# A linear-attention and MLP kernel: batch loads issued after the rest transposes, k loaded ahead of q at the start, group 0's output tiles copied by ScalarE

## The chip, the cores and the metric

The kernel runs on one core of one Trainium2 chip. The metric is the device time of one execution in microseconds; of several runs the median counts. A profiled execution gives the trace from which all durations below are read. Line numbers (L349) are those of the kernel's source. PE is TensorE, DVE is VectorE, ACT is ScalarE, POOL is GpSimd, SP is SyncE; SPq and ACTq are the queues on which SP and ScalarE issue DMAs.

## The reference

Linear attention over 8 batches, 8 heads, 576 positions and a head size of 64, followed by a two-layer MLP over the 4608 tokens (model size 512, inner size 2048):

```python
def phi(x):
    return np.where(x > 0, x, np.exp(x) - 1.0) + 1.0
q_p, k_p = phi(q), phi(k)
kv  = einsum('bhsd,bhse->bhde', k_p, v)
z   = sum(k_p, axis=2)
num = einsum('bhsd,bhde->bhse', q_p, kv)
den = einsum('bhsd,bhd->bhs', q_p, z)[..., None] + 1e-06
x   = (num / den) -> [B * S, H * D]
h   = x @ w_in
out = gelu_tanh(h) @ w_out
```

Inputs and output are float32 in HBM.

## The kernel before

**Tiling.** Each batch of 576 positions is split into a main part of 512 (`MAIN`, four chunks of 128, `C = 4`) and a rest of 64. The main parts of the 8 batches are 8 groups of the MLP (`iteration(j)`, j = 0 to 7). The rests of two batches 2m and 2m + 1 share a tile of 128 (m = 0 to 3), and the four of them make a ninth group (j = 8, `xt_rest`). Batches 0 and 1 (`PAIRED`) take all 576 positions of k and v in one layout; from batch 2 on, the rest keys and values are tiles of their own (`kr`, `vr`), and the rest queries are `qr` for all m.

**What a batch needs before its group.** `exp_of` (ScalarE), `linear_of` and `least_of` (DVE) make phi of q and k; v is cast to bfloat16. `kv_main` or `kv_paired` multiplies k and v on TensorE into `kv_ps`, which `kv_evac` copies to `kvbd`. q is transposed into `qt`. `nab` then multiplies `qt` and `kvbd` into `n_ps` and divides (reciprocal L307, product L309, both on DVE) into x; the tile `n_ps` has one buffer, so one n waits until DVE has read the one before. x is transposed into `xt`. From batch 2 on the transposes of q and x are DMAs on SP's queue (L543, L576), as are those of the rests (`qtr` L589, `xt_rest` L603); for batches 0 and 1 TensorE transposes and ScalarE copies.

**Order.** It is written by hand. A group has 32 slots: 16 h steps (`h_mm`, 4 matmuls, then gelu on ScalarE), then 16 o steps (4 matmuls each into `o_ps`). `at(j, slot, fn)` files work of other batches behind a slot of group j, and `run` emits it there, in the order of filing within a slot. Each engine, and each DMA queue, executes in the order emitted. For a batch b of 4 or more: loads at (b - 3, 18) (for b = 4 at (1, 29)), linear at (b - 2, 13) and after, exp at (b - 2, 15), `least_q` with its four transposes at (b - 2, 17), kv at (b - 1, 2), n at (b - 1, 4), 6, 8 and 10. For the rests m = 1 to 3: load at (2m - 1, 18), exp at (2m, 15), `least` with the transpose `qtr` at (2m, 22), and n at slot 2 of group 4, 5 or 7. So in group 4 the queue of SP gets, in this order, the q transposes of batch 6, the loads of batch 7 (q, k, v, 1 MB each) and the transpose of the rest queries m = 2, whose n stands at (5, 2). The loads of an even batch have four more DMAs, for `kr` and `vr`.

**The start.** SP issues halves of q, k, q, k and then v of batch 0, and behind them the weights. `first_batch` makes phi half by half in the same order, keeps TensorE's clock up with matmuls on a zero tile (`keep_warm`), transposes q on TensorE in two pieces that ScalarE copies to `qt`, and goes on through kv, n, x and the first quarters of h.

**The output.** `finish` copies a tile of 128 x 512 from `o_ps` into half of `o_sb` (`evac`: by DVE for even t, by ScalarE for odd t, in group 0 t = 3 by DVE); a store of 512 KB goes out on ScalarE's queue for each two tiles. In group 0 the o steps run u by u, so the four tiles finish in slots 28 to 31, among the n, the x transposes and the first h quarters of batch 1; its second store is filed at (1, 2).

Of the kernel before, what the change touches and what calls it, by code (L numbers as in the profile page):

```python
# [15 lines left out]
def kernel(  # L16
# [15 lines left out]
    nc = tc.nc  # L32
# [5 lines left out]
    C = 4  # L38
# [35 lines left out]
    def bank(name, shape, dt=FP32):  # L74
        return ps_b.tile(shape, dt, name=name, tag="b")
# [9 lines left out]
    def ld_tile(name, b):  # L85
        shape = [P, NP, J * D] if b in PAIRED and name != "q" else [P, H, C * D]
        ld[name, b] = pld.tile(shape, FP32, name=name + "_x", tag="ld")

    def load_pairs(name, src, b, us=slice(0, NP)):
        s = src[b].rearrange("h s d -> (h s d)").rearrange("(u n f) -> n u f", n=P, f=J * D)  # L90
        nc.sync.dma_start(out=ld[name, b][:, us, :], in_=s[:, us, :])  # L91

    def load_q_paired(b, parities=(0, 1)):
        src = q[b, :, 0:MAIN, :].rearrange("(u a) (p c) d -> p a u (c d)", a=2, c=C)
        for a in parities:
            nc.sync.dma_start(out=ld["q", b][:, NP * a : NP * (a + 1), :], in_=src[:, a])
# [39 lines left out]
    def cast_w_in(i, fn, fs=slice(0, 512)):  # L136
        fn(
            out=w_in_sb[:, :, 512 * i + fs.start : 512 * i + fs.stop],
            in_=w_st[True, i][:, :, fs],
        )  # L140
# [8 lines left out]
    halves = (slice(0, 2), slice(2, 4))  # L149
    for n in "qkv":  # L150
        ld_tile(n, 0)
    for s in range(2):
        load_q_paired(0, (s,))
        load_pairs("k", k, 0, halves[s])
    for s in range(2):
        load_pairs("v", v, 0, halves[s])
    for i in range(4):
# [42 lines left out]
    def by_chunk(t, hs):  # L200
        return t[:, :, hs, :].rearrange("p c h d -> p h c d")

    def phi_tiles(name, b):
        n, hn = ld[name, b].shape[2] // D, ld[name, b].shape[1]
        phi[name, b] = pphi.tile([P, n, hn, D], BF16, name=name + "_p")

    def exp_of(name, b, hs=None):
        x = ld[name, b]
        hs = hs or slice(0, x.shape[1])
        if (name, b) not in exps:  # L210
            exps[name, b] = pe.tile([P, x.shape[2] // D, x.shape[1], D], BF16, name=name + "_e")
        nc.scalar.activation(  # L212
            by_chunk(exps[name, b], hs),
            x[:, hs].rearrange("p h (c d) -> p h c d", d=D),
            AF.Exp,
        )

    def linear_of(name, b, hs=None):
        x = ld[name, b]
        hs = hs or slice(0, x.shape[1])  # L220
        if (name, b) not in phi:
            phi_tiles(name, b)
        nc.vector.tensor_scalar(  # L223
            by_chunk(phi[name, b], hs),
            x[:, hs].rearrange("p h (c d) -> p h c d", d=D),
            1.0,
            1.0,
            op0=ALU.add,
            op1=ALU.max,
        )  # L230

    def least_of(name, b, hs=None):
        p, e = phi[name, b], exps[name, b]
        if hs:
            p, e = p[:, :, hs, :], e[:, :, hs, :]
        nc.vector.tensor_tensor(p, p, e, op=ALU.min)  # L236
# [3 lines left out]
    def cast_v_paired(b, us, fn):  # L240
        fn(
            out=vp_paired(b)[:, :, us, 0:D].rearrange("p j u d -> p u j d"),
            in_=ld["v", b][:, us].rearrange("p u (j d) -> p u j d", d=D),
        )
# [12 lines left out]
    def kv_paired(b, ii, kv_of):  # L257
        kp, vp = phi["k", b], vp_paired(b)
        for j in range(J):
            for s in range(2):  # L260
                for a in range(2):
                    r, u = slice(HP * a, HP * (a + 1)), 2 * ii + s
                    nc.tensor.matmul(  # L263
                        kv_of(a, ii)[HP * s : HP * (s + 1)],
                        lhsT=kp[r, j, u, :],
                        rhs=vp[r, j, u, :],
                        start=(j == 0),
                        stop=(j == J - 1),
                        skip_group_check=True,
                    )  # L270
# [16 lines left out]
    def kv_evac(b, blocks, src, fn):  # L287
        for s in range(2):
            r = slice(HP * s, HP * (s + 1))
            fn(out=kvbds[b % 4][r, blocks, E * s : E * (s + 1)], in_=src[r])  # L290
# [78 lines left out]
    def xt_chunk(j, c):  # L369
        return xts[j][:, :, P * c : P * (c + 1)]  # L370

    def gelu_table():
        nc.scalar.preload_act_table_set("gelu_apprx_tanh_and_others")  # L373
# [3 lines left out]
    def first_batch():  # L377
        w_ps = bank("w_ps", [P, 512])

        def keep_warm(n):  # L380
            for _ in range(n):
                nc.tensor.matmul(w_ps, lhsT=warm[:, 0:P], rhs=warm)  # L382

        qt = pt.tile([P, C, NP, P], BF16, name="qt")
        qs = (slice(0, 4), slice(4, 8))

        def transpose_q(s, fn):
            t_ps = bank("t_ps", [P, C, 2, P], BF16)
            for i in range(2):
                for c in range(C):  # L390
                    h = 4 * s + 2 * i
                    nc.tensor.transpose(
                        t_ps[:, c, i, :], phi["q", 0][:, c, h : h + 2, :], ident
                    )
            fn(out=qt[:, :, 2 * s : 2 * s + 2, :], in_=t_ps)

        keep_warm(18)
        for s in range(2):
            exp_of("q", 0, qs[s])
            exp_of("k", 0, halves[s])  # L400
            linear_of("q", 0, qs[s])
            least_of("q", 0, qs[s])
            linear_of("k", 0, halves[s])
            least_of("k", 0, halves[s])
        transpose_q(0, nc.scalar.copy)
        keep_warm(10)
        transpose_q(1, nc.scalar.copy)
        keep_warm(2)
        for ii in range(2):
            cast_v_paired(0, halves[ii], nc.vector.tensor_copy)  # L410
        for ii in range(2):
            kv_ps = [bank("kv_ps", [P, E]) for _ in range(2)]
            kv_paired(0, ii, lambda a, ii: kv_ps[a])
            for a, fn in enumerate((nc.vector.tensor_copy, nc.scalar.copy)):
                block = slice(2 * a + ii, 2 * a + ii + 1)
                kv_evac(0, block, kv_ps[a].rearrange("p (i e) -> p i e", i=1), fn)
        gelu_table()
        for s in range(2):
            cast_w_in(0, nc.gpsimd.tensor_copy, slice(256 * s, 256 * s + 256))
        for i in range(1, 4):  # L420
            cast_w_in(i, nc.gpsimd.tensor_copy)
        for i in range(2):
            cast_w_out(i, nc.gpsimd.tensor_copy)
        cast_w_out(2, nc.gpsimd.tensor_copy, slice(0, 2))
        keep_warm(2)

        xts[0] = pt.tile([P, NP, MAIN], BF16, name="xt")
        x = {0: nab(qt[:, 0], 0), 1: nab_in_banks(qt[:, 1], 0)}
        for c in range(C):
            transpose_x(x[c], xt_chunk(0, c), nc.scalar.copy)  # L430
            if c + 2 < C:
                x[c + 2] = (nab, nab_in_banks)[c % 2](qt[:, c + 2], 0)
            if c > 0:
                h_quarter(0, c - 1, 3)
        h_quarter(0, C - 1, 3)

    first_batch()


# [3 lines left out]
    def at(j, slot, fn, *args):  # L443
        j, slot = j + slot // 32, slot % 32
        fill.setdefault((j, slot), []).append((fn, args))
# [160 lines left out]
        at(j, s_least, least)  # L606
        at(j_n, 2, n)

    def evac(dst, src, t):
        if t % 2 == 0:  # L610
            nc.vector.tensor_copy(dst, src)  # L611
        else:
            nc.scalar.copy(dst, src)  # L613

    def store_rest(t, o_sb, fs, engs):
        for s in range(2):
# [7 lines left out]
    def finish(j, t, o_ps):  # L624
        if j == B:
            o_sb = pout.tile([P, 2, d_model], FP32, name="o_sb")
            evac(o_sb[:, 0, :], o_ps, t)
            store_rest(t, o_sb, slice(0, d_model), (nc.scalar, nc.sync))
            return
        if t % 2 == 0:  # L630
            o_sbs[j, t // 2] = pout.tile([P, 2, d_model], FP32, name="o_sb")
        o_sb = o_sbs[j, t // 2]
        evac(o_sb[:, t % 2, :], o_ps, 0 if j == 0 and t == C - 1 else t)
        if t % 2 == 1:
            ov = out[j * S : j * S + MAIN, :].rearrange("(p c) f -> p c f", c=C)[:, t - 1 : t + 1]

            def store():
                nc.scalar.dma_start(out=ov, in_=o_sb)

            if j == 0 and t == C - 1:  # L640
                at(1, 2, store)
            else:
                store()
# [65 lines left out]
    for b in range(4, B):  # L709
        plan_prepare(b, (b - 2, 13), (b - 2, 15))  # L710
        if b > 4:
            at(b - 3, 18, load_batch, b)
    for m in range(1, 4):
        at(2 * m - 1, 18, load_rest, "qr", q, m)
        plan_rest(m, 2 * m, 15, 22, (4, 5, 7)[m - 1])
# [37 lines left out]
```

## Time and profile before

| | us |
|---|---|
| median of 3 runs | 298.3 |
| lowest, highest | 298.05, 299.46 |
| the profiled execution | 299.1 |
| its span, first to last instruction | 297.3 |
| TensorE busy (matmul) | 279.2 |
| ScalarE busy | 163.8 |
| DVE busy | 109.2 |
| mean granted clock of TensorE | 0.981 |

The span stands for what the instructions take; 1.8 us of the execution lie outside it. "Busy" is the time in which an engine has an instruction in work. The waits name who waited for whom, with the total, the number and the longest. The chain of work is followed back from the last instruction to what released each step. The granted clock is the share of full speed that TensorE was given in a stretch.

### The profile page before, as it was taken

The page shows a single profiled execution, that of the slowest core. Times are in us where ns is not written, and L with a number is a line of the kernel's source. Part 1 is how long each engine was busy: PE and PEld are TensorE (multiplying, and loading weights), DVE is VectorE, ACT ScalarE, POOL GpSimd, SP SyncE. Part 2 cuts the span into 40 slices and gives each one's busy share as a digit, 9 for nine tenths or more (in the row PEclk, how much of TensorE's full clock was granted, in tenths as well). Part 3 has the DMA queues.
Part 4 walks back from the last instruction along what each step waited for, and adds up shares of the span by engine and source line. Part 5 has one row for each costly group of instructions (what it writes and reads, how often), then busy time and mean ns, then how long its engine had stood idle before and what let it go on. Part 6 is the DMA issues. An engine that isn't in the chain of part 4 may idle for free.

```text
span 297.3 us, 4538 instructions
## 1 busy us (share of the span) xinstructions
PE 279.2 (94%) x1839; PEld 138.4 (47%) x1868; DVE 109.2 (37%) x182; ACT 163.8 (55%) x224; POOL 18.2 (6%) x25
## 2 busy tenths in 40 slices
PE   8799999999999999999999908999999999999994
PEld 3474456445454445444544405544544444444444
DVE  3831468345945625640575003642231010000001
ACT  4866974877867925772578202691564077016500
POOL 5065320000000000000000000000000000000000
PEclk9999999999999999999999966999999999999999
DMA  7999999939789779928992990306150220021022
GB/s 257 410 406 398 411 394 305 358 88 236 124 264 334 158 201 337 192 77 251 313 182 58 275 330 20 71 2 171 76 73 2 87 90 0 0 82 62 0 71 71
DMA packets 71379, 53.76 MB, mean 181 GB/s; under 512 B 42048, under 2 KB 62784, under 8 KB 71360
## 3 DMA queue, kind: packets, MB, share of 16 engines
q1 hardware_dynamic: 68656, 44.58, 51.7%
q10 hardware_dynamic: 2704, 8.91, 8.2%
q8 instruction: 14, 0.23, 0.3%
q14 instruction: 5, 0.04, 0.0%
HBM read 36.70 MB, written 9.44 MB: 155 GB/s over the span
## 4 chain that ended last, share of the span: by engine, by line
PE 84%; DMA 7%; SPq 3%; ACT 2%; DVE 2%; issue 2%; ACTq 0%; DVEq 0%
PE h_ps L349 41%; PE o_ps L647 37%; DMA qtr<-qr_p 4%; PE n_ps L294 3%; DMA v_x<-in_v_dram 3%; SPq L543 2%; PE kv_ps L278 2%; SPq L100 1%; ACT q_e L212 1%; PE t_ps L341 1%; SPq L91 0%; DVE x L309 0%; DVE o_sb L611 0%; ACT L212 0%; PE kv_ps L263 0%
## 5 line engine op out<-in xcount | busy, mean ns | idle before, releaser
L647 PE MATMUL o_ps<-w_out_sb,g 128*128 128x512 bf16 (+1 forms) x581 | 126.2, 373 | 1.0 <-ACT w_out_sb L143 0.2
L349 PE MATMUL h_ps<-xt,w_in_sb 128*128 128x512 bf16 (+1 forms) x556 | 118.0, 359 | 1.2 <-issue 0.4
L359 ACT ACTIVATE g<-h_ps 128x512 bf16<-128x512 f32 x144 | 85.0, 597 | 57.1 <-PE h_ps L349 53.0
L647 PEld LDWEIGHTS <-g 128*128 128x128 bf16 x592 | 57.7, 98 | 65.3 <-issue 0.3
L349 PEld LDWEIGHTS <-w_in_sb 128*128 128x128 bf16 x636 | 57.8, 98 | 60.5 <-issue 2.4
L613 ACT COPY o_sb<-o_ps 128x512 f32<-128x512 f32 (+1 forms) x17 | 9.7, 573 | 60.2 <-PE o_ps L647 53.1
L611 DVE COPY o_sb<-o_ps 128x512 f32<-128x512 f32 (+1 forms) x20 | 13.5, 676 | 69.4 <-PE o_ps L647 69.4
L307 DVE RECIPROCAL r<-n_ps 128x8 f32<-128x8 f32 x34 | 7.0, 207 | 59.4 <-PE n_ps L294 59.4
L309 DVE TENSOR_TENSOR x<-n_ps,r 128x512 bf16<-128x512 f32 x34 | 23.5, 691 | 1.2
L212 ACT ACTIVATE q_e<-q_x 128x2048 bf16<-128x2048 f32 (+1 forms) x9 | 15.5, 1721 | 2.8 <-DMA q_x<-in_q_dram 2.8
L212 ACT ACTIVATE k_e<-k_x 128x2048 bf16<-128x2048 f32 (+2 forms) x9 | 15.8, 1755 | 0.7 <-DMA k_x<-in_k_dram 0.7
L236 DVE TENSOR_TENSOR q_p<-q_p,q_e 128x2048 bf16<-128x2048 bf16 (+1 forms) x9 | 9.9, 1105 | 15.5 <-ACT q_e L212 15.3
L223 DVE TENSOR_SCALAR q_p<-q_x 128x2048 bf16<-128x2048 f32 (+1 forms) x9 | 10.0, 1106 | 14.2 <-DMA q_x<-in_q_dram 14.2
L349 PE MATMUL h_ps<-xt_rest,w_in_sb 128*128 128x512 bf16 x63 | 13.9, 379 | 0.1
L294 PEld LDWEIGHTS <-qt 128*128 128x128 bf16 x128 | 9.7, 98 | 7.5 <-DVE x L309 1.1
L294 PE MATMUL n_ps<-kvbd,qt 128*128 128x130 bf16 x128 | 12.7, 221 | 0.3 <-DVE x L309 0.3
L223 DVE TENSOR_SCALAR k_p<-k_x 128x2048 bf16<-128x2048 f32 (+2 forms) x9 | 10.2, 1133 | 5.5 <-DMA k_x<-in_k_dram 5.5
L236 DVE TENSOR_TENSOR k_p<-k_p,k_e 128x2048 bf16<-128x2048 bf16 (+2 forms) x9 | 11.0, 1226 | 0.9 <-ACT k_e L212 0.7
L382 PE MATMUL w_ps<-warm 128*128 128x512 bf16 x31 | 9.9, 477 | 1.3 <-DVE warm L177 1.2
L290 DVE CAST kvbd<-kv_ps 64x260 bf16<-64x260 f32 (+2 forms) x18 | 6.6, 366 | 10.9 <-PE kv_ps L278 8.3
L373 ACT ACT_TABLE_LOAD x8 | 10.3, 1283 | 0.1
L212 ACT ACT_TABLE_LOAD x8 | 10.3, 1283 | 0.1
(49 smaller groups left out, 96.4 us busy)
## 6 DMA issues: line engine op xcount, KB each, us to landing
out_dram<-o_sb ACTq DMA_DIRECT2D x16, 512.0 KB, 3.3
q_x<-in_q_dram SPq DMA_DIRECT2D x6, 1024.0 KB, 6.3
k_x<-in_k_dram SPq DMA_DIRECT2D x6, 1024.0 KB, 10.0
v_x<-in_v_dram SPq DMA_DIRECT2D x6, 1024.0 KB, 7.7
w_st<-in_moe_w_in_dram SPq DMA_DIRECT2D x4, 1024.0 KB, 14.6
w_st<-in_moe_w_out_dram SPq DMA_DIRECT2D x4, 1024.0 KB, 13.6
q_x<-in_q_dram SPq DMA_DIRECT2D x4, 512.0 KB, 8.7
k_x<-in_k_dram SPq DMA_DIRECT2D x2, 576.0 KB, 5.6
```

Source lines behind the costliest of these rows:

```text
L212: nc.scalar.activation(by_chunk(exps[name, b], hs), x[:, hs].rearrange("p h (c d) -> p h c d", d=D), AF.Exp,)
L223: nc.vector.tensor_scalar(by_chunk(phi[name, b], hs), x[:, hs].rearrange("p h (c d) -> p h c d", d=D), 1.0, 1.0, op0=ALU.add, op1=ALU.max,)
L236: nc.vector.tensor_tensor(p, p, e, op=ALU.min)
L294: nc.tensor.matmul(ns[i // 2][rows, 2 * E * (i % 2) : 2 * E * (i % 2 + 1)], lhsT=qt_c[:, i, rows], rhs=kvbd[:, i, :], skip_group_check=True,)
L309: nc.vector.tensor_tensor(x_view(x, paired), n_v[:, :, :, 0:D], r[:, :, :, None].to_broadcast([P, 2, NP, D]), op=ALU.mult,)
L349: nc.tensor.matmul(h_ps[:, ts], lhsT=w_in_sb[:, c, P * m : P * (m + 1)], rhs=xt[:, c, ts], start=(c == 0), stop=(c == KM - 1), skip_group_ ...
L359: nc.scalar.activation(g[:, m, :], h_ps, AF.Gelu_apprx_tanh)
L373: nc.scalar.preload_act_table_set("gelu_apprx_tanh_and_others")
L382: nc.tensor.matmul(w_ps, lhsT=warm[:, 0:P], rhs=warm)
L611: nc.vector.tensor_copy(dst, src)
L613: nc.scalar.copy(dst, src)
L647: nc.tensor.matmul(o_ps, lhsT=g[:, m, P * t : P * (t + 1)], rhs=w_out_sb[:, m, fs], start=(m == 0), stop=(m == MM - 1),)
```

## The change

Three edits. The loads of batches 5, 6 and 7 are filed at slot 23 instead of slot 18 of group b - 3, so behind the rest transpose of slot 22. In the start, each half of k is loaded ahead of the half of q, and phi is made in that order, with exp, linear and least of one piece together. In group 0, the tiles t = 0, 1 and 2 are copied by ScalarE and t = 3 by DVE, and both stores are filed at (1, 2). For the other groups the copies are as before.

```diff
     for s in range(2):
+        load_pairs("k", k, 0, halves[s])
         load_q_paired(0, (s,))
-        load_pairs("k", k, 0, halves[s])
...
         for s in range(2):
-            exp_of("q", 0, qs[s])
-            exp_of("k", 0, halves[s])
-            linear_of("q", 0, qs[s])
-            least_of("q", 0, qs[s])
-            linear_of("k", 0, halves[s])
-            least_of("k", 0, halves[s])
+            for n, hs in (("k", halves[s]), ("q", qs[s])):
+                exp_of(n, 0, hs)
+                linear_of(n, 0, hs)
+                least_of(n, 0, hs)
...
-    def evac(dst, src, t):
-        if t % 2 == 0:
-            nc.vector.tensor_copy(dst, src)
-        else:
-            nc.scalar.copy(dst, src)
+    def evac(dst, src, on_scalar):
+        (nc.scalar.copy if on_scalar else nc.vector.tensor_copy)(dst, src)
...
     def finish(j, t, o_ps):
         if j == B:
...
-            evac(o_sb[:, 0, :], o_ps, t)
+            evac(o_sb[:, 0, :], o_ps, t % 2)
...
-        evac(o_sb[:, t % 2, :], o_ps, 0 if j == 0 and t == C - 1 else t)
+        evac(o_sb[:, t % 2, :], o_ps, t < C - 1 if j == 0 else t % 2)
...
-            if j == 0 and t == C - 1:
+            if j == 0:
                 at(1, 2, store)
             else:
                 store()
...
     for b in range(4, B):
         plan_prepare(b, (b - 2, 13), (b - 2, 15))
         if b > 4:
-            at(b - 3, 18, load_batch, b)
+            at(b - 3, 23, load_batch, b)
```

## The prediction

> **What bounds the kernel now.** I read the page first, then TensorE's waits, longest first, then the chain of work that ended last. The page, its engine rows and clock row, and the waits:
>
> ```profile
> PE 279.2 (94%) x1839; PEld 138.4 (47%) x1868; DVE 109.2 (37%) x182; ACT 163.8 (55%) x224; POOL 18.2 (6%) x25
> PEclk9999999999999999999999966999999999999999
> PE n_ps L294 <- DMA qtr<-qr_p: 8.5, 1, 8.5
> PE n_ps L294 <- DVE x L309: 0.3, 1, 0.3
> PE h_ps L349 <- ACT xt L342: 0.2, 1, 0.2
> ```
>
> TensorE is busy for 94% of the span, so only its gaps and its slow stretches can be won. One wait is 8.5 us, for the transposed rest queries (tile qtr), and the two slices with a lower clock lie at the same place. The next two waits that the change could touch are 0.3 and 0.2 us. The chain around the long wait (start, length, what):
>
> ```profile
> 164.87 0.59 SPq L100
> ...
> 166.18 1.43 SPq L100
> 167.71 11.34 DMA qtr<-qr_p
> 179.09 0.66 PE n_ps L294 x8
> ```
>
> SP's line 100 is `load_main`: SP issues the loads of batch 7 from 164.87 and only then, at 167.71, the transpose of the rest queries of batches 4 and 5 (m = 2). It lands 11.34 us later, and TensorE starts 0.04 us after that. The cost of this is read by laying the stretch beside its twin one group earlier, from the group's first h matmuls to the first n matmuls of slot 4 (columns: stretch, length, busy time of PE, PEld, DVE, ACT, POOL, granted clock, DMA share, GB/s):
>
> ```profile
> 138.32:143.75 5.43, 5.38 (x71) 2.90 (x70) 1.66 (x4) 2.97 (x5) 0.00 (x0) 1.00 1.04 321
> 167.83:184.17 16.34, 7.61 (x71) 4.04 (x71) 1.75 (x4) 2.97 (x5) 0.00 (x0) 0.69 0.69 224
> 138.32:167.83 29.51, 29.35 (x191) 14.24 (x191) 14.57 (x25) 18.04 (x24) 0.00 (x0) 1.00 0.84 207
> 167.83:208.41 40.58, 31.75 (x191) 15.45 (x193) 12.47 (x19) 17.00 (x22) 0.00 (x0) 0.87 0.46 135
> 179.09:184.17 5.08, 4.86 (x58) 2.96 (x60) 1.75 (x4) 0.60 (x1) 0.00 (x0) 0.53 0.13 29
> ```
>
> The same 71 matmuls take 5.43 us in group 4 and 16.34 us in group 5: 10.91 us too many. Of these 8.5 are the wait; the other 2.4 are the restart, 5.08 us at a granted clock of 0.53. Whole groups say 40.58 - 29.51 = 11.07.
>
> **Part 1: loads of batches 5 to 7 from slot 18 to slot 23.** Moved are 3 DMAs for batch 5, 7 for batch 6 (its rest keys and values too), 3 for batch 7, all on SP's queue. Between the two slots that queue holds, in groups 2 and 4, one rest transpose (slot 22), and in group 3 the two loads of `load_rest("qr", q, 2)`. ScalarE's queue, which holds the stores, and POOL's are not touched. So the transpose for m = 2 goes out in front of 3 MB instead of behind it. When would it land? First the rows of the timeline, then of DMA issues, where the last number is the time to landing (of the transposes at 84.23 and at 167.71):
>
> ```profile
> 84.23 1.21 SPq L589 DMA_TRANSPOSE qtr<-qr_p  x1
> 85.55 0.52 SPq L100 DMA_DIRECT2D q_x<-in_q_dram  x1
> 161.87 0.43 DVE L236 TENSOR_TENSOR qr_p<-qr_p,qr_e 128x512 bf16<-128x512 bf16 x1
> 167.83 2.75 PE L349 MATMUL h_ps<-xt,w_in_sb 128*128 128x512 bf16 x12
> ```
> ```profile
> qtr<-qr_p SPq DMA_TRANSPOSE x1, 2.3
> qtr<-qr_p SPq DMA_TRANSPOSE x1, 11.3
> ```
>
> Its data is ready at 161.87 + 0.43 = 162.30, so it would take the place of the first load at 164.87. At 84.23 the program already has this very order, a rest transpose with a batch load 1.3 us behind it, and it landed in 2.3 us. That gives 167.2. TensorE asks for it at 167.83 + 2.75 = 170.58, so 3.4 us are in hand. The bounds are that row and the blocked one, 11.3 us, which would land at 176.2; I take the near one, since no load stands ahead of it in this place. The wait goes, the clock has no reason to fall, and the term is **-10.9** (11.07 by whole groups).
>
> On the restart there is a rule to weigh. The Trainium skill, "TensorE: Matmul & The Clock Gate", Part 1, says that the array falls to half its clock after about 3.4 us without work and is released after about 3.4 us of work. By it the restart costs 3.4 x 0.5 = 1.7 us (an estimate from that page), and the term is 8.5 + 1.7 = 10.2 rather than 10.9. The trace's stretch is longer than the page's, 5.08 us at 0.53, and decides.
>
> What is late next? The loads themselves: each goes out one transpose later (1.21 us by the row above), batch 6's two small loads later (1.67 below). Rows for the last load of batch 7 (time to landing), then the work that needs it and what the engines do next:
>
> ```profile
> v_x<-in_v_dram SPq DMA_DIRECT2D x1, 1024.0 KB, 12.2
> ```
> ```profile
> 145.69 1.67 SPq L118 DMA_DIRECT2D qr<-in_q_dram  x2
> 158.07 1.22 DVE L236 TENSOR_TENSOR q_p<-q_p,q_e 128x2048 bf16<-128x2048 bf16 x1 [2.71 <-ACT q_e L212]
> 193.44 1.22 DVE L247 CAST vp<-v_x 128x2048 bf16<-128x2048 f32 x1
> 198.49 1.23 DVE L236 TENSOR_TENSOR q_p<-q_p,q_e 128x2048 bf16<-128x2048 bf16 x1 [3.82 <-ACT q_e L212]
> ```
>
> Batch 7's v lands at 166.18 + 12.2 + 1.2 = 179.6; its cast, 10.9 earlier than now, stands at 182.5. That is 2.9 us of cover, and behind the cast DVE idles 3.82 us waiting for ScalarE's exponentials, 6.7 us in all. For batch 6, 1.67 us of delay lies below the 2.71 us of that idle time. Cost 0; without the cover each us late would hold `least_of` and the output copies behind it on DVE, and TensorE only when the banks run out.
>
> **Part 2: k ahead of q.** The four half loads change places; the bytes in front of v do not change. The last pieces (chain first, then timeline):
>
> ```profile
> 3.36 8.30 DMA v_x<-in_v_dram
> 11.68 0.77 DVE vp L241
> ```
> ```profile
> 10.15 0.76 DVE L236 TENSOR_TENSOR k_p<-k_p,k_e 128x1152 bf16<-128x1152 bf16 x1
> 8.68 0.69 DVE L236 TENSOR_TENSOR q_p<-q_p,q_e 128x1024 bf16<-128x1024 bf16 x1
> 10.21 0.61 PE L392 MATMUL t_ps<-ident,q_p 128*128 128x128 bf16 x8
> 9.87 2.00 ACT L395 COPY qt<-t_ps 128x1024 bf16<-128x1024 bf16 x2
> 13.35 0.76 PE L294 MATMUL n_ps<-kvbd,qt 128*128 128x130 bf16 x8
> ```
>
> The second half of v lands at 11.66 and its cast follows at once; that, not q or k, sets the opening. DVE ends with the last of the four pieces at 10.91 today; with q last, whose piece is no longer (0.69 beside 0.76), by 10.9 too. Its eight transposes (0.61) then end near 11.5 and the second copy to qt, 1.0 us, near 12.5. The n matmuls that need it start at 13.35: 0.8 us of cover. Term **0**, bounds -0.1 (q's pieces are shorter, so DVE is free for v's first half a little sooner) and +0.5 (that copy, half of it, pushes ScalarE's kvbd copies in front of n).
>
> **Part 3: group 0's output tiles.** ScalarE copies t = 0, 1, 2, DVE t = 3; the store of t = 0, 1 (512 KB) moves behind that of group 1's third step, on ScalarE's own queue.
>
> ```profile
> 44.48 0.40 PE L294 MATMUL n_ps<-kvbd,qt 128*128 128x130 bf16 x4
> 44.69 0.69 DVE L611 COPY o_sb<-o_ps 128x512 f32<-128x512 f32 x1 [0.27 <-PE o_ps L647]
> 44.95 1.03 PE L647 MATMUL o_ps<-w_out_sb,g 128*128 128x512 bf16 x4
> 45.29 0.20 DVE L307 RECIPROCAL r<-n_ps 128x8 f32<-128x8 f32 x1
> 46.01 0.58 ACT L613 COPY o_sb<-o_ps 128x512 f32<-128x512 f32 x1 [0.28 <-PE o_ps L647]
> 46.27 0.41 PE L294 MATMUL n_ps<-kvbd,qt 128*128 128x130 bf16 x4 [0.30 <-DVE x L309]
> ```
>
> DVE's copy of t = 0 (44.69 to 45.38) holds up the reciprocal, whose input is there at 44.88. Without it the reciprocal, x and so the n matmuls at 46.27 come 0.34 earlier; TensorE is busy until 44.95 + 1.03 = 45.98, so it wins its 0.30 us wait. On ScalarE two copies of 0.58 come in; each ends before the xt copy behind it is asked for, or delays it by at most 0.1, and h needs that chunk over 1 us later. The last wait, 0.2 us for xt, I let stay: nothing that is taken off DVE stands between it and TensorE's own transposes. The second store adds one issue in a later slot, where ScalarE has idle time between gelus. Term **-0.3**, bounds -0.4 and +0.6 (one ScalarE copy in full on the path).
>
> **Sum.** 299.1 us (profiled execution: span 297.3 and 1.8 around it) - 10.9 + 0 - 0.3 = 287.9. The median of the runs shown is 298.3, 0.8 below the profiled one; the sum on it is 287.1. Whether those 0.8 lie in the stall I can't see, so I take the middle, **287.5**.
>
> **The rivals.** (a) The transpose goes out first but lands late, held by the load packets behind it or the store at ScalarE's queue. For: the blocked row. Against: 2.3 us in the same order at 84.23. From 3.4 us of delay on it costs one for one; 0.5 to 3.5 us of wait give 288 to 291. (b) The opening or the ScalarE copies cost their upper bounds, 0.5 and 0.9 more than taken: up to 288.9. (c) The change does not act: the transpose meets another obstacle (data or semaphore) and TensorE waits as now: 298 to 298.6. Against: its data is ready 2.6 us before its turn. (d) Slower: the loads, now later, hold SP, and the x transposes of group 5 queue behind them until group 6 starves. Their price is read from group 4, which starts at 138.32 with batch 6's seven loads on the queue:
>
> ```profile
> 149.86 5.96 SPq L576 DMA_TRANSPOSE xt<-x  x4
> ```
>
> There the four x transposes are issued by 155.82, 17.5 us after the group's start. From 167.5 that is 185.0, with 1.2 of delay 186.2; group 6 starts at 208.41 - 11.2 = 197.2. That is 11 us of cover less a landing; only a delay beyond it costs, and it takes 11.2 us more to eat the gain and 1.5 more to show: 300 or above. The Trainium skill, "DMA: Bandwidth & Descriptors", Rules for kernel authors, speaks for this rival in advising to issue transfers early; no row here shows such a shortage.
>
> **How the numbers follow.** A difference under 0.5%, 1.5 us, is about what can't be told from none. Likeliest, as summed: 0.83, with 286.5 to 288.6. (a) 0.07, (b) 0.05, both still faster; (c) 0.03; (d) 0.02. Faster 0.95, within 0.5% 0.03, slower 0.02. The range takes in (b) and the near half of (a): 286.3 to 289.6.
>
> **What would show it.** Right: no wait of n for qtr, its landing within 4 us of issue and ahead of batch 7's loads, group 5 at about 29.5 us, granted clock 1.00 there, and no wait of n for DVE's x near 46. Wrong: a wait of n, of h for xt at group 6, or of DVE for batch 7's v that reaches TensorE; an opening in which v's cast is not the last link; or a low clock at another place.

## The result, and the profile after

| | before | after |
|---|---|---|
| median of 4 runs, us | 298.88 | 288.95 |
| lowest, highest | 298.05, 299.82 | 288.86, 289.24 |
| profiled execution | 299.1 | 288.86 |
| its span | 297.3 | 286.9 |

The changed kernel is faster: ratio 0.9669, 95% interval 0.9634 to 0.9704. The forecast was 287.5 with a range of 286.3 to 289.6; the measured time lies inside it, 1.45 us above the forecast.

The page and TensorE's waits of the changed kernel (who waited for whom, total, times, longest):

```profile
PE 278.5 (97%) x1868; PEld 137.0 (48%) x1868; DVE 107.8 (38%) x180; ACT 164.7 (57%) x226; POOL 18.4 (6%) x25
PEclk9999999999999999999999999999999999999999
...
PE t_ps L392 <- DVE q_p L236: 1.6, 2, 0.9
...
PE h_ps L349 <- ACT xt L342: 0.2, 1, 0.2
```

The wait for qtr and the two slices with a low clock are gone. So is the wait of n for x, of 0.3 us. The wait of h for xt stays. A wait that was not among those of before, of the first batch's transposes for q, is the longest now; it is not on the chain. TensorE's busy time has hardly changed (279.2 to 278.5): the gain lies in time in which it waited or ran slowly.

The same stretches as before, by stage (columns as in the prediction):

```profile
138.67:168.34 29.67, 29.67 (x193) 14.35 (x192) 14.58 (x25) 18.04 (x24) 0.00 (x0) 1.00 0.86 207
168.34:198.00 29.66, 29.66 (x193) 14.31 (x192) 12.38 (x19) 17.00 (x22) 0.00 (x0) 1.00 0.73 189
168.34:173.76 5.42, 5.42 (x71) 2.90 (x70) 1.66 (x4) 2.97 (x5) 0.00 (x0) 1.00 0.88 272
```

Group 5 takes as long as group 4, and its first stretch 5.42 us, where the twin took 5.43. (Before, the boundary between the two groups, 167.83, was 0.16 us early, since it was the start of an h matmul while the last o matmul still ran; group 4 was 29.67 there too and group 5 40.42.) How qtr got there, timeline first, then its DMA with the time to landing:

```profile
162.21 0.43 DVE L236 TENSOR_TENSOR qr_p<-qr_p,qr_e 128x512 bf16<-128x512 bf16 x1
165.34 1.21 SPq L587 DMA_TRANSPOSE qtr<-qr_p  x1
166.60 0.58 SPq L100 DMA_DIRECT2D q_x<-in_q_dram  x1
170.85 0.44 PE L294 MATMUL n_ps<-kvbd,qtr 128*64 128x130 bf16 x8
177.63 5.15 SPq L574 DMA_TRANSPOSE xt<-x  x4
183.03 1.22 DVE L247 CAST vp<-v_x 128x2048 bf16<-128x2048 f32 x1
```
```profile
qtr<-qr_p SPq DMA_TRANSPOSE x1, 2.4
```

It goes out in front of the load, lands at 167.7, and n takes it at 170.85 without a wait.

The chain in the opening, the changed kernel's:

```profile
3.36 8.96 DMA v_x<-in_v_dram
12.35 0.77 DVE vp L241
```

The second half of v lands at 12.32 instead of 11.66. And around the end of group 0:

```profile
45.15 0.40 PE L294 MATMUL n_ps<-kvbd,qt 128*128 128x130 bf16 x4
45.35 0.58 ACT L608 COPY o_sb<-o_ps 128x512 f32<-128x512 f32 x1 [1.11 <-PE o_ps L642]
45.59 0.21 DVE L307 RECIPROCAL r<-n_ps 128x8 f32<-128x8 f32 x1 [0.50 <-PE n_ps L294]
46.58 0.41 PE L294 MATMUL n_ps<-kvbd,qt 128*128 128x130 bf16 x4
```

The two n are 1.43 us apart, where they were 1.79 (44.48 and 46.27). The span's 10.4 us come out as: opening +0.66, group 0 -0.36, group 2 +0.05, group 5 -10.76.

### The profile page after: what moved, and what is told of

The parts are those of the page before. It is cut to its first block, busy times and chain, and to the rows that moved or that the text cites. A ratio compares the mean times of both kernels' runs of the same rounds, so it can differ in the third digit from the quotient of the medians.

```text
span 286.9 us, 4569 instructions
## 1 busy us (share of the span) xinstructions
PE 278.5 (97%) x1868; PEld 137.0 (48%) x1868; DVE 107.8 (38%) x180; ACT 164.7 (57%) x226; POOL 18.4 (6%) x25
## 4 chain that ended last, share of the span: by engine, by line
PE 93%; DMA 3%; DVE 1%; SPq 1%; ACT 1%; issue 0%; ACTq 0%
PE h_ps L349 44%; PE o_ps L642 43%; DMA v_x<-in_v_dram 3%; PE n_ps L294 3%; PE kv_ps L278 1%; PE t_ps L341 1%; SPq L91 1%; PE kv_ps L263 0%; SPq L96 0%; PE t_ps L469 0%; DVE x L330 0%; DVE vp L241 0%; DVE x L309 0%; ACT w_out_sb L143 0%; ACT xt L342 0%
## 5 line engine op out<-in xcount | busy, mean ns | idle before, releaser
L608 ACT COPY o_sb<-o_ps 128x512 f32<-128x512 f32 (+1 forms) x19 | 10.9, 574 | 61.5 <-PE o_ps L642 54.4
L608 DVE COPY o_sb<-o_ps 128x512 f32<-128x512 f32 (+1 forms) x18 | 12.1, 674 | 69.0 <-PE o_ps L642 69.0
L236 DVE TENSOR_TENSOR k_p<-k_p,k_e 128x2048 bf16<-128x2048 bf16 (+2 forms) x9 | 10.2, 1132 | 1.4 <-ACT k_e L212 1.4
```

Source lines behind the costliest of these rows:

```text
L608: (nc.scalar.copy if on_scalar else nc.vector.tensor_copy)(dst, src)
```

## The experiments

Times are medians, with the lowest and highest run in brackets. The experiments fall into three sets; in each the kernel before ran on the same chip beside the others. Theory A says that the new order at the start costs the 0.66 us there; rival B that it is the spread of the transfers from execution to execution.

**First set (before: 298.83).** The start put back:

```diff
 for s in range(2):
-    load_pairs("k", k, 0, halves[s])
     load_q_paired(0, (s,))
+    load_pairs("k", k, 0, halves[s])
...
-    for n, hs in (("k", halves[s]), ("q", qs[s])):
-        exp_of(n, 0, hs) ...
+    exp_of("q", 0, qs[s])
+    exp_of("k", 0, halves[s]) ...
```

> The changed kernel with the start as it was: q's halves loaded and worked ahead of k's. Theory A (the new order costs the opening its time): v's last half lands near 11.7 us instead of 12.3, the h matmuls start 0.66 us earlier, and the time falls by 0.66 to about 288.3. Rival B (the 0.66 us is the spread of DMA from execution to execution): the time stays at about 288.9 and v's landing differs between executions of either order.

Measured 288.11 (287.97 to 288.52); ratio to before 0.9637 (0.9615 to 0.9659). The chain of this kernel:

```profile
3.42 8.21 DMA v_x<-in_v_dram
11.65 0.77 DVE vp L241
```

Group 0's tiles put back:

```diff
-evac(o_sb[:, t % 2, :], o_ps, t < C - 1 if j == 0 else t % 2)
+evac(o_sb[:, t % 2, :], o_ps, (0 if t == C - 1 else t % 2) if j == 0 else t % 2)
...
-            if j == 0:
+            if j == 0 and t == C - 1:
```

> The changed kernel with group 0's tiles copied and stored as before. Theory (the copies on ScalarE are worth the wait of n for x): the wait of 0.30 us near 46 is back and the time rises by 0.36 to about 289.3. Rival (the earlier store or other things matter more): no change, 288.9, or a rise above 0.6. Its opening is that of the changed kernel, a second look at when v lands: theory A says 12.3 again, rival B some other value between 11.6 and 12.4.

Measured 289.40 (289.23 to 289.53). The wait of n for x is back at 0.3 us, v lands at 12.33 as in the first profile.

Of the three edits only the loads, on the kernel before (`at(b - 3, 23, load_batch, b)`):

> The kernel before with the loads of batches 5 to 7 moved to slot 23 alone. Theory (all of the large gain is the wait of n for qtr and the restart behind it): no such wait, group 5 in 29.7 us instead of 40.4, clock 1.00; 10.8 us off the time of before, about 288.3 beside 299.1. Rival (the three edits work together): more than 1 us away from this.

Measured 288.79 (288.54 to 288.96), no wait for qtr: 10.0 us under the kernel before. And the base of the set, the changed kernel as it is:

> The changed kernel once more, as the base of this call. 288.9 us. Theory A: v's last half lands at 12.3 again (k's second half at 8.05). Rival B: v lands elsewhere between 11.6 and 12.4, and the time moves with it.

Measured 288.70 (288.63 to 288.82), v landing at 11.96. So the changed kernel is 0.59 us slower than the one with the old start, in ranges that don't overlap: theory A has the sign and the size. But v's landing differs by 0.36 us between two executions of the same program, so B holds for a part of what one profile shows.

The old tiles cost 0.70 beside this base, by the letter of what was expected (a rise above 0.6) a sign for the rival. In the two profiles 0.37 of it is the later landing (12.33 beside 11.96) and 0.33 lies in group 0. But the kernel with the old start and the one with only the loads moved differ in the tiles alone, v lands at 11.63 and 11.64 in them, and they are 0.68 apart as well (288.11 and 288.79), of which group 0 of their profiles shows 0.48. So the tiles are worth 0.3 to 0.5 us in the profiles and perhaps more in the medians; where the rest lies is not shown.

**Second set (before: 299.21).** The loads back at slot 18 in the changed kernel:

> The changed kernel with the loads back at slot 18. Theory (the loads are the gain): n for m = 2 waits for qtr again by 8 to 9 us, the clock falls to half behind it, and the time is 299 to 299.5 (before, plus 0.66 of the opening, less 0.36 of the tiles). Rival (the other edits hold part of the gain): clearly under 298.

Measured 299.21, ratio 1.0006 (0.9989 to 1.0023): without the moved loads the other two edits give nothing that can be measured. TensorE's wait in this kernel:

```profile
PE n_ps L294 <- DMA qtr<-qr_p: 8.6, 1, 8.6
```

The same order reached from the other side, on the kernel before: `plan_rest(m, 2 * m, 15, 17, ...)` in place of `22`, the loads untouched at slot 18.

> The kernel before with the loads left at slot 18, and the work on the rest queries (linear, least and the transpose qtr) moved up from slot 22 to slot 17, so that qtr is ahead of the loads on SP's queue. Theory (only the order of qtr and the loads counts): as with the moved loads, no wait for qtr, about 288.3. Rival (the later loads themselves help, by leaving the DMA engines to other transfers): a wait or other loss remains, 290 or more.

Measured 288.48 (288.31 to 288.68), no wait for qtr. So it isn't the slot of the loads that counts, but which of the two goes out first.

The price of the restart by itself, on the kernel before, in `plan_rest`:

```diff
         def n():
+            if m == 2:
+                w_ps = bank("w_ps", [P, 512])
+                for _ in range(38):
+                    nc.tensor.matmul(w_ps, lhsT=warm[:, 0:P], rhs=warm)
             n_ps = pair_of_banks("n_ps")
```

> The kernel before with 38 matmuls on a zero tile in front of the n of m = 2, into a bank of their own: they run while TensorE waits for qtr (about 8.2 us at 0.216 each). Theory (the loss of 10.8 us is a wait of 8.5 and a restart at half clock): the wait for qtr's landing stays, the clock stays at 1.00, and the time falls by the 2.3 of the restart, to about 296.6. Rival (the restart costs nothing of its own, the slow matmuls only stand beside other waits): 298.9.

Measured 298.00 (297.05 to 298.35), ratio 0.9953 (0.9937 to 0.9970). That is between theory and rival: the medians fall by 1.2 us, half of what was expected. The profiled execution, the fastest of the five, was 297.05, against 299.1 before. Its chain, and its stretches (length, then busy times, clock after the fifth pair):

```profile
167.59 11.59 DMA qtr<-qr_p
179.17 0.04 issue
179.22 0.43 PE n_ps L294 x8
...
182.12 0.23 PE n_ps L294 x4
```
```profile
171.00:179.00 8.00, 7.82 (x37) 3.30 (x34) 0.00 (x0) 0.25 (x1) 0.00 (x0) 1.00 0.98 321
179.22:182.12 2.90, 2.90 (x59) 1.91 (x60) 1.66 (x4) 0.60 (x1) 0.00 (x0) 1.00 0.09 21
```

qtr lands as late as before (11.59 beside 11.34 us), but TensorE, kept busy, stays at full clock, and the restart takes 2.90 us instead of 5.08. So between these two executions the restart at half clock costs 2.18 us of its own, and the wait 8.5: together 10.7, which is the 10.76 of group 5 within 0.1. Why the medians show only 1.2 us is open; in the four other runs of this kernel no trace shows when qtr landed.

Only batch 7's loads moved, on the kernel before (`at(b - 3, 23 if b == B - 1 else 18, load_batch, b)`):

> The kernel before with only batch 7's loads moved to slot 23; batches 5 and 6 stay at 18. Theory (of the three moved loads only batch 7's is in front of a transpose that is asked for soon): the whole 10.8 us, about 288.3. Rival (the loads of batches 5 and 6 count too): 288.8 or more.

Measured 288.72 (288.51 to 289.95). SP's queue in group 3 of this kernel:

```profile
111.90 3.07 SPq L100 DMA_DIRECT2D v_x<-in_v_dram  x1
115.07 3.87 SPq L589 DMA_TRANSPOSE qtr<-qr_p  x1
119.03 1.22 SPq L603 DMA_TRANSPOSE xt_rest<-x  x1
```

Here the transpose for m = 1 still stands behind batch 5's loads, but its n comes a whole group later; nothing waits. The time is 0.4 above the theory's and just under the rival's 288.8, but v lands at 12.00 in this profile, 0.36 later than with all three loads moved, and against the kernel before beside it the gain is 10.5 us, where all three gave 10.0. So no part of the gain is seen that needs the loads of batches 5 and 6.

**Third set (before: 298.76).** Which half of the edit at the start costs? First the loads k first, but the work q first:

> The changed kernel with only the work of the first batch put back (phi of q ahead of k); the loads stay k first. So far v's last half landed at 11.6 to 12.0 with q first (six profiles) and at 12.0 to 12.3 with k first (four). Theory A1 (the order of the loads slows the transfers): v lands at 12.0 to 12.3. Theory A2 (the order of the work beside them does): 11.6 to 11.8. In both the work on k now ends the opening's chain, about 1 us later than in the changed kernel: 289.5 to 290.

Measured 290.63 (290.59 to 290.81). Then the loads q first and the work k first:

> The opposite half: the loads of the first batch q first again, the work still k ahead of q. A1: v lands at 11.6 to 11.8. A2: 12.0 to 12.3. ScalarE waits for k's first half with nothing to do, so the work on q ends about 1 us later than with q worked first: about 289.

Measured 289.61 (289.44 to 289.91). In both the chain runs through the phi work, so v's landing doesn't set the time, but it can be read: v's second half lands at 12.3 with k loaded first and at 11.6 with q loaded first, as A1 said, in one execution each. Over all profiles it lands at 11.6 to 12.0 with q loaded first and at 12.0 to 12.3 with k first, so the two orders touch.

The rate of the transfers differs as well. The stretch 5 to 8 us (last number GB/s, before it the share of the DMA engines' time), in this order: before, changed, k loaded first with the work q first, q loaded first with the work k first.

```profile
5.00:8.00 3.00, 3.00 (x18) 1.46 (x17) 2.48 (x5) 2.45 (x3) 0.00 (x0) 1.00 1.06 398
```
```profile
5.00:8.00 3.00, 2.28 (x13) 0.96 (x12) 2.27 (x4) 1.64 (x2) 0.28 (x1) 1.00 1.05 367
```
```profile
5.00:8.00 3.00, 2.63 (x15) 1.15 (x14) 1.70 (x3) 2.10 (x2) 0.00 (x0) 1.00 1.05 370
```
```profile
5.00:8.00 3.00, 2.30 (x10) 0.83 (x8) 1.59 (x3) 2.02 (x2) 0.00 (x0) 1.00 1.07 400
```

In this stretch the rate follows the order of the loads, not of the work: 398 to 400 GB/s in the nine profiled executions with q loaded first, 335 to 372 in the five with k first. But that is not enough to make v late. Between 2 and 5 us it is the other way round (308 GB/s before, 334 changed), and over both stretches together the two kernels, before and changed, move nearly the same:

```profile
2.00:8.00 6.00, 6.00 (x25) 2.52 (x24) 2.89 (x5) 2.87 (x4) 2.67 (x8) 1.00 0.97 353
```
```profile
2.00:8.00 6.00, 5.28 (x20) 2.02 (x19) 2.85 (x4) 2.24 (x3) 3.17 (x8) 1.00 1.01 351
```

What does separate the orders is how far v's own packets are drawn out. By the packet records of the traces the first packet of v starts at 8.20 us before and at 7.98 in the changed kernel, so not later; its last one ends at 11.34 and at 12.03. Over all profiles that is 3.0 to 3.4 us from v's first packet to its last with q loaded first, and 3.7 to 4.1 with k first. The weights behind v on the queue start at 10.9 in both, and by the end of v 70 KB of them have moved before and 302 KB in the changed kernel. So a part of v comes late while the queue already carries what stands behind it. Why the order does this was not found. In the kernel with the old tiles the rate has its part too: 332 GB/s over 2 to 8 us, where the thirteen other profiles have 345 to 360.

Both times were 0.6 us above what was expected. With q loaded first and k worked first, most of that is the opening: its first h matmuls start at 18.01 us, 1.40 later than in the kernel with the old start (16.61), where 1 us was expected. With k loaded first and q worked first they start at 18.28, 0.98 later than in the changed kernel (17.30), as expected, and the excess lies elsewhere: the profiled execution has a span of 287.9 and 2.9 us outside it, the other runs 288.5 to 288.8 and 1.8 to 2.1, so the one profile doesn't show all of it, and what it is stays open.

Two kernels put together what helped. One gets qtr ahead of the loads by slots 17 and 18, with the old start and the new tiles:

> What helped, put together in another way: the start as before (q first), the tiles of group 0 on ScalarE, and the rest work with its transpose moved up to slot 17 in front of loads that stay at slot 18. Theory (only the order of transpose and loads counts): the same as with the loads moved, 288.1. Rival (earlier issue of the loads is worth something): below 287.9.

Measured 288.23 (287.80 to 288.31): the earlier issue of the loads is worth nothing that shows. The other is the changed kernel with the old start again:

> The changed kernel with the start as it was, once more beside the others of this call. Theory A: 288.1 again, 0.6 under the changed kernel's 288.7 to 288.95, with v landing at 11.6 to 11.8. Rival B (spread of DMA): a time nearer to 288.7, v landing at 12.0 or later.

Measured 288.09 (287.96 to 289.09), v landing at 11.63; ratio to before 0.9646 (0.9624 to 0.9669). This kernel beats both: it was 0.59 us under the changed one beside it in the first set, and is 0.86 under that one's first 288.95, across sets. What to ship is the moved loads and the tiles, without the new start.

## Why the prediction was right, step by step

- **The wait and the restart** (taken: -10.9, by the twin stretch). Measured -10.76. The parts: the wait 8.5 as the row said; the restart 2.18 by the profile of the kernel with the matmuls in the wait, where 2.4 was taken as the rest of 10.91 (its median gives only 1.2). The 0.16 us of a group boundary read early is most of the difference. The Trainium skill's rule ("TensorE: Matmul & The Clock Gate", Part 1) gave 1.7 for the restart, as an estimate; this profile shows 0.5 more.
- **qtr's landing** (taken: 2.3 us, from the one place that had the order already). Measured 2.4; in hand were 3.1 us instead of 3.4. The rival of a late landing did not come about, nor the one in which the change doesn't act.
- **The loads, later** (taken: 0). Right, with less cover than stated: v of batch 7 lands at 181.3 (issued 167.90, 13.4 us to landing), not 179.6, and its cast starts at 183.03; 1.7 us of cover instead of 2.9. The issue came 0.5 us later than taken, and the time to landing, carried over from the old order as 12.2, was 1.2 longer. The x transposes of group 5 are issued by 182.78, 15 us before group 6 starts at 198.00: the slower rival was far off.
- **k ahead of q** (taken: 0, bounds -0.1 and +0.5). This step failed: it costs 0.66 us in the profile and 0.59 between the medians of one set, above its upper bound. The premise was that as many bytes in front of v mean the same landing. But v, on which the opening does hang, landed 0.66 us later: its packets took 4.1 us from first to last instead of 3.1, though nearly as many bytes had moved between 2 and 8 us; the cause of that stays open. The bound was worked out on the work of ScalarE and DVE, the wrong resource; the second qt copy, the suspect, ends at 13.20 in front of n at 14.02, with its cover. That the time lies inside the range owes to the room left there for rivals (a) and (b), not to this step.
- **Group 0's tiles** (taken: -0.3). Measured -0.36 in the profile; between kernels that differ in the tiles alone 0.33 and 0.48 in group 0 of their profiles, and 0.68 where the medians can be compared at the same landing of v. So the mechanism held, and the size may have been taken too small. The xt wait of 0.2 us stayed, as said.
- **The sum.** 287.9 was forecast for the profiled execution and 288.86 came: +0.66 from the start, +0.14 from the stall, -0.06 from the tiles, +0.05 in group 2, and 1.96 instead of 1.8 us outside the span. The other 0.5 of the miss is mostly the step from the profiled execution to the median: 0.8 us lay between them before, by the three runs known then (0.2 with the fourth), and I gave half of it to the kernel after. With no wait for qtr the runs lie within 0.4 us, and the median is 0.09 above the profiled one.

## What to carry to other kernels

On one DMA queue, look for a small transfer that someone waits for soon, filed behind large ones that are needed late; swapping them cost nothing that shows here and gave 10.8 us in the profile, 10.0 in the medians of the kernel with that edit alone. Price a stall by a twin stage without it, which counts the slow restart too. Where the last link of a chain is a transfer, equal bytes in front of it are not equal time: read its landing in the new order from a run, or keep the order.

## What the runs showed of the hardware

- The order of the same loads changes when the one behind them lands. With halves of q of 512 KB (pieces of 1 KB in each row) ahead of halves of k of 576 KB (2.3 KB), the packets of v took 3.0 to 3.4 us from first to last, in nine executions; with k ahead, 3.7 to 4.1, in five. The bytes moved between 2 and 8 us were nearly the same in the profiles before and after (353 and 351 GB/s).
- After a wait of 8.5 us the restart cost 2.18 us, in one pair of executions; TensorE kept busy through the same wait had a granted clock of 1.00.
- The spread went with the wait. The kernels that wait for qtr spread by 1.3 to 1.9 us over their runs (before, the loads back at slot 18, the matmuls in the wait); those that don't by 0.2 to 0.6, but for one run each of the kernel with only batch 7's loads moved and of the second one with the old start, some 1 us above its fellows; in these two the extra time lies outside the span (2.9 us instead of 1.8 to 2.1). That the waits for qtr make the spread fits this and was not tried.
